# Values of two sequences loaded plainly by SyncE and cast by VectorE, in an attention kernel with a leaky-ReLU layer behind it

## The chip, the cores and the metric

The kernel runs on one core of one Trainium2 chip. The metric is the device time in microseconds (us) of one execution. The profile adds one execution taken by the hardware profiler. Its engines are TensorE (PE in the profile, with PEld for its weight loads), VectorE (DVE), ScalarE (ACT), GpSimd (POOL) and SyncE (SP). GpSimd and SyncE also issue transfers; their issues are instructions on their own in-order queues.

## What is computed

Attention over eight sequences of 576 tokens with eight heads of 64 values, each with 16 extra "beacon" keys and values that every token may see; then two matrix products with a leaky ReLU between them. Inputs and output are fp32.

```python
B, H, S, Nb, D = (8, 8, 576, 16, 64)
k_all = np.concatenate([beacon_k, k], axis=2)
v_all = np.concatenate([beacon_v, v], axis=2)
scores = np.matmul(q, k_all.transpose(0, 1, 3, 2)) / np.sqrt(D)
scores = np.where(causal, -1e9, scores)          # the beacon columns are never masked
a = softmax(scores)
x = np.matmul(a, v_all)                          # then heads side by side: 4608 x 512
h = x @ w_in                                     # 512 -> 2048
out = np.maximum(0.01 * h, h) @ w_out            # 2048 -> 512
```

## The kernel before

**Units of work.** A *pair* g is two heads of one sequence; g // 4 is the sequence, so pairs 0 to 3 belong to sequence 0, 4 to 7 to sequence 1, 8 to 11 to sequence 2. For each pair, TensorE makes the scores in transposed form (`score`, L256, for pairs 0 to 7; `block` and `stretch`, L299 and L774, in blocks of three 512-column tiles over all later pairs), ScalarE takes the exponential into `aT`, GpSimd blanks the upper triangle (`triangle`, L287), and TensorE multiplies with the values (`value`, two halves; L359). The values carry a column of ones, so the same product gives the sum that VectorE divides by (L388, L389) into `x_nat`. Two halves of a pair's value product: half 0 takes query tiles 0 to 2 and so key chunks 0 to 2; half 1 takes tiles 3 and 4 and all five chunks.

**Values.** `v_bufs` are two bf16 buffers, for even and odd sequences. `load_v_cast` (L205) fills one of five 128-row chunks with a transfer that GpSimd issues and that turns fp32 into bf16 on the way; chunk 0 takes a second small one for the 16 beacon rows. So a sequence takes six issues.

**Queries and keys.** Pairs 0 to 7 come in through `load_qk` (tile `gsum`) and are turned by TensorE. From pair 8 on, GpSimd loads them as `q_nat` and `k_nat` (`load_natural`, L167) and SyncE turns them by transposing transfers (`turn_pair`, L177), into `qT` and into the tile `kT`, which has eight key buffers. `beacon_columns` (L227) then copies the 16 beacon keys of a pair into the first columns of its key buffer, on GpSimd (L229).

**The layer behind.** Its input `xT` is filled by TensorE transposes and a copy (`finish`, L672, by way of `x_transposes`) or by SyncE's transposing transfers (`x_turn`, L412). The tokens are taken in nine chunks of 512. `up` makes one of 16 slices of the hidden layer (L442), which ScalarE writes to the tile `gT` (L450), of which there are two in turn; `down` makes a part of the output (L512 for chunk 0; L537 later). From chunk 1 on, the output product goes by sums of weight blocks (`weight_sums`, L455, three subtractions on VectorE) and of tokens (L610).

**What sets the order.** Each engine runs its instructions in the order in which the code issues them. For sequences 0 and 1 that order is written out by hand in strings that `run` (L680) reads (L739 to L758). A step is a letter and numbers: `s` a score tile, `m` its mask, `v` a value half, `x` a finish, `y` an `x_turn`, `q` and `k` turning by TensorE, `l` a `load_qk`, `N` a `load_natural` half, `T` a `turn_pair`, `V` a value chunk (`V1.0` is sequence 1, chunk 0), `i` and `o` halves of `w_in` and `w_out`, `b` a beacon copy, `t` the weight sums, `u` and `d` an `up` and a `down`. From sequence 2 on, events with a due time in units of pairs are sorted (L785 to L808) and slices of the layer are filled in between. Completion of transfers is counted on eight semaphores for GpSimd's and eight for SyncE's, used in turn, so an issue also waits until the eighth issue before it is done.

Of the kernel before, what the change touches and what calls it, by code (L numbers as in the profile page):

```python
# [8 lines left out]
FP32 = mybir.dt.float32  # L9
BF16 = mybir.dt.bfloat16  # L10
# [5 lines left out]
def kernel(  # L16
# [11 lines left out]
    nc = tc.nc  # L28

    B, H, S, D = q.shape  # L30
    NB = beacon_k.shape[2]
# [6 lines left out]
    NF = DF // 128  # L38
# [7 lines left out]
    NKB = 5  # L46
    ROWS = [128, 128, 128, 128, 80]
    OFF = [0, 112, 240, 368, 496]
# [31 lines left out]
    gpool = ctx.enter_context(tc.tile_pool(name="gpool", bufs=2))  # L80
# [21 lines left out]
    v_bufs = [singles.tile([128, NKB, H, D + 1], BF16, name=f"v_aug{i}") for i in range(2)]  # L102
# [102 lines left out]
    def load_v_cast(b, c):  # L205
        dst = v_bufs[b % 2]
        lo = 0
        if c == 0:
            nc.gpsimd.dma_start(
                out=dst[0:NB, 0, :, 0:D], in_=beacon_v[b].rearrange("h p d -> p h d")  # L210
            )
            lo = NB
        n = ROWS[c] - lo
        nc.gpsimd.dma_start(  # L214
            out=dst[lo : ROWS[c], c, :, 0:D],
            in_=v[b, :, OFF[c] : OFF[c] + n].rearrange("h p d -> p h d"),
        )

    def operand(g, which):
# [62 lines left out]
    def mask(g, part):  # L282
        aT = probs[g]
        for lo, n, rows in MASKS[part]:
            triangle(aT, lo, n, rows)
# [82 lines left out]
    def value_ahead(g):  # L368
        if (g, 0) not in avs:
            avs[g, 0] = ps_one.tile([128, 512], FP32, name="av", tag="one")  # L370
        value_matmuls(g, 0, avs[g, 0][:, 0:396].rearrange("p (n w) -> p n w", w=66), (0, 1))
        begun.add(g)
# [56 lines left out]
    gT = {}  # L429
# [242 lines left out]
    def finish(g, eng=0):  # L672
        if eng < 2 and g in xs:
            x_transposes(g, (dve, act)[eng])
        ready[0] = chunks_with(g)
        if g % NPAIR == NPAIR - 1:
            turn[0] = 1
            held[0] = LEAD

    def run(steps):  # L680
        for step in steps.split():
            op, a = step[0], [int(x) for x in step[1:].split(".")] if step[1:] else []
            if op == "s":
                score(*a)
            elif op == "m":
                mask(*a)
            elif op == "v":
                value(*a)
            elif op == "e":
                value_ahead(*a)  # L690
            elif op == "x":
                finish(*a)
            elif op == "l":
                load_qk(*a)
            elif op == "V":
                load_v_cast(*a)
            elif op == "N":
                load_natural(*a)
            elif op == "T":
                turn_pair(a[0])  # L700
            elif op == "y":
                x_turn(a[0])
            elif op == "q" or op == "k":
                t_q(a[0], 0 if op == "q" else 1, (dve, act)[a[1] if len(a) > 1 else 0])
            elif op == "b":
                beacon_columns(a[0], (dve, act, pool)[a[1]])
            elif op == "u":
                up()
            elif op == "d":
                down()  # L710
            elif op == "w":
                unused(*a)
            elif op == "W":
                unused_ahead(*a)
            elif op == "i":
                load_w_in(a[0])
            elif op == "o":
                load_w_out(a[0])
            elif op == "t":
                weight_sums(a[0])  # L720
            else:
                raise ValueError(step)
# [11 lines left out]
    with order:  # L734
        load_first_keys()
        load_beacon_k(0, 2, nc.scalar)
        nc.vector.memset(blank, 0.0)
        nc.vector.memset(ident, 0.0)
        run("l0.0 l1.0")  # L739
        make_identity(nc, ident, nomemset=True)  # L740
        make_ones()
        run("l1.1 l2.0 l2.1 V0.0 V0.1 l3.0 l3.1 V0.2 V0.3 V0.4 l4.0 l4.1 i0")
        make_pads()
        unused(13, 256)
        cast_beacon_k(0, 2, nc.scalar.copy)
        beacon_transposes(0, 2)
        unused(13)
        nc.scalar.copy(out=k_nat0[:, :, 0], in_=first_k[0])
        nc.vector.tensor_copy(out=k_nat0[:, :, 1], in_=first_k[1])
        run("q0.1 k0 w2.384 s0.0 m0.0 w3.256 s0.1 q1 s0.2 m0.1 k1 s0.3 m0.2")  # L750
        run("w2.384 s1.0 m1.0 q2 s1.1 k2 w2.384 s1.2 m1.1 w2.384 s1.3 m1.2 W0.0.4 s2.0 m2.0 W0.0.4 s2.1 W0.0.6 q3 l5.0 l5.1 s2.2 k3 w4.384 v0.0 m2.1 s2.3 i1 m2.2 W0.1.4 s3.0 m3.0 v1.0 s3.1 v0.1 s3.2 v1.1 m3.1 l6.0 l6.1 s3.3 x0.1 m3.2")
        run("v2.0 V1.0 V1.1 q4 v2.1 x1 k4.1 v3.0 v3.1 x2.1 s4.0 s4.1 x3 m4.0 V1.2 V1.3 V1.4 l7.0 l7.1 u u s4.2 s4.3 q5 k5 m4.1 m4.2 u o0 u")
        load_beacon_k(2, B, nc.gpsimd)
        run("s5.0 s5.1 m5.0 u u u s5.2 s5.3 q6 k6 m5.1 m5.2 o1 u u s6.0 s6.1 m6.0 u v4.0 u v4.1 y4 N8.0 N8.1 u s6.2 s6.3 q7 k7 m6.1 m6.2 u")
        cast_beacon_k(2, B, nc.gpsimd.tensor_copy)
        run("u v5.0 u v5.1 N9.0 s7.0 s7.1 m7.0 d x5 v6.0 v6.1 T8 d s7.2 s7.3")
        beacon_transposes(2, B)
        run("m7.1 m7.2 N9.1 u b8.2 b9.2 b10.2 b11.2 x6 v7.0 T9 v7.1 d d t0 d N10.0 N10.1 d V2.0 V2.1 x7 T10")  # L758


        FIRST = 2 * NPAIR
        COLS = FLAT[NKB]
        TILES = (NG - FIRST) * COLS // 512

        def tile_parts(n):
            at, end, parts = 512 * n, 512 * (n + 1), []
            while at < end:
                r, lo = divmod(at, COLS)
                hi = min(COLS, lo + end - at)
                parts.append((FIRST + r, lo, hi))  # L770
                at += hi - lo
            return parts

        def block(m):  # L774
            tiles = [tile_parts(n) for n in range(3 * m, min(3 * m + 3, TILES))]
            for n, parts in enumerate(tiles):
                stretch(parts, apart=n == 0)
            for parts in tiles:
                triangles(parts)

        def has_down():
            return at2[0] < done1[0] // NF

        since = 0
        events = []  # L785
        for g in range(FIRST, NG):
            if g > FIRST + 2:
                events.append((g - 2.75, 0, run, ("N%d.0" % g,)))
                events.append((g - 2.45, 0, run, ("N%d.1" % g,)))
            if g > FIRST + 2:  # L790
                events.append((g - 1.75, 0, run, ("T%d" % g,)))
            if g > FIRST + 3:
                events.append((g - 1.65, 0, run, ("b%d.2" % g,)))
            at = g + (2.05 if g % NPAIR == NPAIR - 1 else 2.25)
            events.append((at, 3, value, (g, 0)))
            events.append((at + 0.37, 4, value, (g, 1)))
            events.append((at + 0.38, 5, x_turn, (g,)))
        for m in range((TILES + 2) // 3):
            events.append((FIRST + (0.4 if m else 0.6) + 1536 / COLS * m, 2, block, (m,)))
        ends = [FIRST]  # L800
        for g in range(FIRST, NG):
            events.append((g + 3.5, 2, finish, (g, 2)))
            if g % NPAIR == NPAIR - 1:
                ends.append(g + 3.5)
        for b in range(2, B):
            for n in range(2 if b == 2 else 0, NKB):
                events.append((4 * b + (-0.4 if b == 2 else -0.9) + 0.3 * n, 6, load_v_cast, (b, n)))
        events.sort(key=lambda e: e[:2])  # L808
        first_down[0] = 4
        w, d0 = 0, done1[0] + done2[0]  # L810
        for at, _, what, args in events:
            while w + 2 < len(ends) and at > ends[w + 1]:
                w, d0 = w + 1, done1[0] + done2[0]
            todo = NF * ready[0] + sum(ND(i) for i in range(ready[0])) - KEPT - d0
            aim = d0 + todo * (at - ends[w]) / (ends[w + 1] - ends[w])
            while done1[0] + done2[0] < aim and fill():
                pass
            if what is block:
                since = done1[0] + done2[0]
            elif what is value:  # L820
                while done1[0] + done2[0] < since + (2 if has_down() else 4) and fill(True):
                    pass
            what(*args)
        while at2[0] < NCH:
            fill()
# [30 lines left out]
```

## Time and profile before

| | |
|---|---|
| three runs | 330.48, 332.94, 335.08 us |
| the profiled execution | 333.21 us, of which the profile's span is 331.5 |
| mean granted TensorE clock in it | 0.995 |
| values, issue to landing (128 KB chunks, median) | 7.1 us |
| keys and queries of a pair, issue to landing (72 KB, median) | 4.6 to 4.9 us |
| transposing transfers, issue to landing (median) | 4.6 to 4.8 us |

Two parts of the page:

```profile
ACT  4969862588753885477756784686467516553510
POOL 8795868979997697567748877697221000000000
PEclk9999999999997999999999999999999999999999
DMA  8999999999999999999999999999321111000103
...
q0 software_dynamic: 99824, 18.54, 85.2%
q1 hardware_dynamic: 55792, 20.77, 36.8%
```

The first four rows cut the span into 40 slices of 8.3 us; a digit is the busy share in tenths, or the granted clock. The other two rows are the transfer queues: q0 is fed by GpSimd, q1 by SyncE, and both run on the same 16 transfer engines; packets, megabytes and the time of the packets as a share of 16 engines. In the timelines quoted below, a line gives the start, the time taken, engine, source line and operation, how many instructions it merges, and in brackets the idle time of the engine before it and what ended it.

### The profile page before, as it was taken

How to read it: one execution, taken by the hardware profiler on the slowest of the kernel's cores; microseconds unless marked ns; L12 is line 12 of the kernel's file. 1: busy time of each engine (PE TensorE's matmuls, PEld its weight loads, DVE VectorE, ACT ScalarE, POOL GpSimd, SP SyncE). 2: the span in 40 equal slices, each digit the busy share in tenths (PEclk: the TensorE clock that was granted, in tenths of full speed). 3: DMA queues.
4: the chain of work that ended last, by engine and by line, in shares of the span. 5: the costliest groups of instructions: out<-in, count | busy, mean ns of one | idle time of the engine just before them, and what ended most of it. 6: DMA issues, size and time to landing. Idle time of an engine off the chain costs nothing.

```text
span 331.5 us, 8537 instructions
## 1 busy us (share of the span) xinstructions
PE 319.8 (96%) x3429; PEld 213.5 (64%) x3429; DVE 145.9 (44%) x297; ACT 200.1 (60%) x336; POOL 187.5 (57%) x354
## 2 busy tenths in 40 slices
PE   7999999899969999999999999999999999999995
PEld 4574555355657457855688888557865684566685
DVE  3563346307534254435434535443543552424344
ACT  4969862588753885477756784686467516553510
POOL 8795868979997697567748877697221000000000
PEclk9999999999997999999999999999999999999999
DMA  8999999999999999999999999999321111000103
GB/s 134 127 202 184 131 208 126 179 165 154 139 134 141 169 134 132 154 137 149 133 138 146 120 131 140 187 128 117 87 97 51 36 52 63 2 33 32 65 32 129
DMA packets 155928, 39.93 MB, mean 120 GB/s; under 512 B 143040, under 2 KB 153152, under 8 KB 155888
## 3 DMA queue, kind: packets, MB, share of 16 engines
q0 software_dynamic: 99824, 18.54, 85.2%
q1 hardware_dynamic: 55792, 20.77, 36.8%
q8 instruction: 27, 0.44, 0.6%
q14 instruction: 13, 0.11, 0.1%
q10 hardware_dynamic: 272, 0.07, 0.1%
HBM read 37.22 MB, written 9.44 MB: 141 GB/s over the span
## 4 chain that ended last, share of the span: by engine, by line
PE 67%; DMA 16%; ACT 4%; POOL 4%; DVE 4%; issue 3%; SPq 1%; DVEq 0%; ACTq 0%; POOLq 0%
PE acc L442 28%; PE acc L537 25%; PE av L359 6%; PE sc L314 5%; DMA gsum<-in_q_dram 5%; DMA xT<-x_nat 3%; DMA w_out_sb<-in_moe_w_out_dram 3%; DMA v_aug<-in_v_dram 3%; ACT aT L333 3%; PE acc L512 2%; DMA k_nat<-in_k_dram 2%; POOL aT L289 1%; DVE p L559 1%; DVE u L559 1%; POOL gsum L158 1%
## 5 line engine op out<-in xcount | busy, mean ns | idle before, releaser
L442 PE MATMUL acc<-xT,w_in_sb 128*128 128x512 bf16 (+1 forms) x640 | 136.8, 358 | 1.4 <-DMA xT<-x_nat 0.5
L450 ACT ACTIVATE gT<-acc 128x512 bf16<-128x512 f32 x144 | 83.5, 617 | 54.0 <-PE acc L442 51.5
L289 POOL TENSOR_SCALAR_AFFINE_SELECT aT<-aT 128x256 bf16<-128x256 bf16 (+2 forms) x160 | 64.0, 429 | 55.3 <-ACT aT L329 34.1
L442 PEld LDWEIGHTS <-w_in_sb 128*128 128x128 bf16 x640 | 59.4, 98 | 52.6 <-issue 4.2
L537 PEld LDWEIGHTS <-gT 128*128 128x128 bf16 x512 | 49.5, 99 | 9.1 <-issue 1.0
L333 ACT ACTIVATE aT<-sc 128x1024 bf16<-128x1024 f32 (+3 forms) x64 | 51.8, 895 | 2.0 <-PE sc L314 2.0
L537 PE MATMUL acc<-w_out_sb,gT 128*128 128x256 bf16 x384 | 47.9, 279 | 0.0
L359 PEld LDWEIGHTS <-aT 128*128 128x128 bf16 (+1 forms) x960 | 36.6, 98 | 9.4 <-DVE x_nat L389 1.5
L537 PEld LDWEIGHTS <-gsum 128*128 128x128 bf16 x384 | 36.7, 98 | 6.7
L359 PE MATMUL av<-v_aug,aT 128*128 128x65 bf16 (+1 forms) x960 | 39.5, 194 | 1.1 <-DVE x_nat L389 0.5
L329 ACT ACTIVATE aT<-sc 128x512 bf16<-128x512 f32 (+3 forms) x64 | 29.0, 522 | 18.4 <-PE sc L314 18.4
L562 ACT COPY p<-acc 128x512 f32<-128x512 f32 (+1 forms) x25 | 14.5, 581 | 41.2 <-PE acc L537 37.6
L388 DVE RECIPROCAL rec<-av 128x6 f32<-128x6 f32 (+1 forms) x64 | 11.9, 187 | 56.1 <-PE av L359 55.8
L214 POOL DMA_DIRECT2D v_aug<-in_v_dram x40 | 34.0, 855 | 4.1 <-DMA w_in_sb<-in_moe_w_in_dram 3.3
L171 POOL DMA_DIRECT2D k_nat<-in_k_dram x48 | 34.8, 729 | 1.0 <-issue 0.9
L171 POOL DMA_DIRECT2D q_nat<-in_q_dram x48 | 34.8, 731 | 0.7
L389 DVE TENSOR_TENSOR x_nat<-av,rec 128x384 bf16<-128x384 f32 (+1 forms) x64 | 31.4, 490 | 2.2
L537 PE MATMUL acc<-w_sum,gsum 128*128 128x256 bf16 x256 | 31.9, 273 | 0.0
L276 ACT ACTIVATE aT<-sc 128x1024 bf16<-128x1024 f32 (+3 forms) x32 | 26.0, 875 | 5.1 <-PE sc L267 5.0
L314 PE MATMUL sc<-qT,kT 64*128 64x80 bf16 (+22 forms) x384 | 22.2, 250 | 3.3 <-POOL kT L229 2.7
L610 DVE TENSOR_TENSOR gsum<-gT 128x1024 bf16<-128x1024 bf16 x16 | 11.2, 697 | 30.1 <-ACT gT L450 30.1
L314 PEld LDWEIGHTS <-kT 64*128 64x128 bf16 x384 | 13.0, 94 | 15.1 <-issue 8.7
(62 smaller groups left out, 225.1 us busy)
## 6 DMA issues: line engine op xcount, KB each, us to landing
out_dram<-p SPq DMA_DIRECT2D x26, 256.0 KB, 2.4
q_nat<-in_q_dram POOLq DMA_DIRECT2D x48, 72.0 KB, 4.6
k_nat<-in_k_dram POOLq DMA_DIRECT2D x48, 72.0 KB, 4.9
v_aug<-in_v_dram POOLq DMA_DIRECT2D x24, 128.0 KB, 7.1
w_in_sb<-in_moe_w_in_dram POOLq DMA_DIRECT2D x2, 1024.0 KB, 11.9
w_out_sb<-in_moe_w_out_dram POOLq DMA_DIRECT2D x2, 1024.0 KB, 11.7
out_dram<-u SPq DMA_DIRECT2D x8, 256.0 KB, 2.4
gsum<-in_q_dram POOLq DMA_DIRECT2D x8, 144.0 KB, 6.6
```

Source lines behind the costliest of these rows:

```text
L171: nc.gpsimd.dma_start(out=t[:, :, par], in_=(q, k)[which][b, 2 * hp + par].rearrange("(t p) d -> p t d", p=NR),)
L214: nc.gpsimd.dma_start(out=dst[lo : ROWS[c], c, :, 0:D], in_=v[b, :, OFF[c] : OFF[c] + n].rearrange("h p d -> p h d"),)
L276: nc.scalar.activation(out=aT[:, :, c0 : c0 + w], in_=sc[:, :, 0:w], func=AF.Exp, scale=0.125)
L289: nc.gpsimd.affine_select(out=view, in_=view, compare_op=ALU.is_ge, fill=0.0, base=128 - n if lo == 0 else 0, channel_multiplier=-1, patte ...
L314: nc.tensor.matmul(out=(sc[par] if apart else sc[:, par])[:, at : at + b - a], lhsT=kT[ps_, c * 128 : (c + 1) * 128], rhs=qT[ps_, q0 : q0 ...
L329: nc.scalar.activation(out=probs[g][:, par, lo:hi], in_=sc[par][:, at : at + hi - lo], func=AF.Exp, scale=0.125)
L333: nc.scalar.activation(out=probs[g][:, :, lo:hi], in_=sc[:, :, at : at + hi - lo], func=AF.Exp, scale=0.125)
L359: nc.tensor.matmul(out=avv[:, n, 0 : D + 1], lhsT=aT[0 : ROWS[c], par, a0 : a0 + 128], rhs=va[0 : ROWS[c], c, 2 * hp + par, :], start=(c = ...
L389: nc.vector.tensor_tensor(out=x_nat[:, t0:t1].rearrange("p t e d -> p (t e) d"), in0=avv[:, :, 0:D], in1=rec[:, n0:n1, None].to_broadcast( ...
L442: nc.tensor.matmul(out=acc[:, lo:hi], lhsT=w_in_cols(fc, j), rhs=xT[:, j, x0 : x0 + hi - lo], start=(j == 0), stop=(j == NJ - 1), skip_gro ...
L450: nc.scalar.activation(out=gT[i][:, fc, :], in_=acc, func=AF.Prelu, alpha=0.01)
L537: nc.tensor.matmul(out=acc[:, lo : lo + HD], lhsT=left(i, n, fc, tile), rhs=right(n, fc), start=(lo == 0 and fc == 0), stop=(fc == HF - 1) ...
```

## The change

The values of sequences 1 and 2 no longer come through `load_v_cast`. Five steps `L` (`load_v_plain`) have SyncE bring the fp32 values, unchanged in type, into `gT[1]`, the hidden-layer tile of chunk 1, which is not written before the end of the hand-written part; it is cut into eight staging places. A step `G` (`gate_v`) writes two zeros into each place on VectorE, and SyncE's load waits for that. Five steps `C` (`cast_v`) have VectorE copy the values into the bf16 buffer. Sequence 1 is gated behind `v3.0`, and cast behind `k6`; sequence 2 is gated behind `x5`, and cast at the end of the hand-written part.

Besides, one `u` moves from before `s6.2` to before `v4.0`, the weight sums `t0` and the finish `x7` change places so that `t0` stands behind `x7`, and a beacon copy is due 2.5 units before its pair rather than 1.65. Sequences 3 to 7 keep the old loads.

```diff
+    def gate_v(*slots):
+        for i in range(2):
+            if i not in gT:
+                gT[i] = gpool.tile([128, NF, 512], BF16, name="gT")
+        for n in slots:
+            nc.vector.memset(stage(n)[:, 0:1, 0:2], 0.0)
+
+    def stage(n):
+        return gT[1][:, 2 * n : 2 * n + 2].rearrange("p f t -> p (f t)").bitcast(FP32).rearrange(
+            "p (h d) -> p h d", d=D
+        )
+
+    def load_v_plain(b, c, n):
+        t = stage(n)
+        lo = 0
+        if c == 0:
+            nc.sync.dma_start(out=t[0:NB], in_=beacon_v[b].rearrange("h p d -> p h d"))
+            lo = NB
+        nc.sync.dma_start(
+            out=t[lo : ROWS[c]], in_=v[b, :, OFF[c] : OFF[c] + ROWS[c] - lo].rearrange("h p d -> p h d")
+        )
+        staged[b, c] = n
+
+    def cast_v(b, c):
+        nc.vector.tensor_copy(
+            out=v_bufs[b % 2][0 : ROWS[c], c, :, 0:D], in_=stage(staged[b, c])[0 : ROWS[c]]
+        )
...
-        run("v2.0 V1.0 V1.1 q4 v2.1 x1 k4.1 v3.0 v3.1 x2.1 s4.0 s4.1 x3 m4.0 V1.2 V1.3 V1.4 l7.0 l7.1 u u s4.2 s4.3 q5 k5 m4.1 m4.2 u o0 u")
+        run("v2.0 q4 v2.1 x1 k4.1 v3.0 G0.4.1.2.6 L1.0.0 L1.1.4 L1.2.1 L1.3.2 L1.4.6 v3.1 x2.1 s4.0 s4.1 x3 m4.0 l7.0 l7.1 u u s4.2 s4.3 q5 k5 m4.1 m4.2 u o0 u")
         load_beacon_k(2, B, nc.gpsimd)
-        run("s5.0 s5.1 m5.0 u u u s5.2 s5.3 q6 k6 m5.1 m5.2 o1 u u s6.0 s6.1 m6.0 u v4.0 u v4.1 y4 N8.0 N8.1 u s6.2 s6.3 q7 k7 m6.1 m6.2 u")
+        run("s5.0 s5.1 m5.0 u u u s5.2 s5.3 q6 k6 C1.0 C1.1 C1.2 C1.3 C1.4 m5.1 m5.2 o1 u u s6.0 s6.1 m6.0 u u v4.0 u v4.1 y4 N8.0 N8.1 s6.2 s6.3 q7 k7 m6.1 m6.2 u")
...
-        run("u v5.0 u v5.1 N9.0 s7.0 s7.1 m7.0 d x5 v6.0 v6.1 T8 d s7.2 s7.3")
+        run("u v5.0 u v5.1 N9.0 s7.0 s7.1 m7.0 d x5 G3.7.2.6.5 L2.0.3 L2.1.7 L2.2.2 L2.3.6 L2.4.5 v6.0 v6.1 T8 d s7.2 s7.3")
...
-        run("m7.1 m7.2 N9.1 u b8.2 b9.2 b10.2 b11.2 x6 v7.0 T9 v7.1 d d t0 d N10.0 N10.1 d V2.0 V2.1 x7 T10")
+        run("m7.1 m7.2 N9.1 u b8.2 b9.2 b10.2 b11.2 x6 v7.0 T9 v7.1 d d d N10.0 N10.1 d x7 t0 C2.0 C2.1 C2.2 C2.3 C2.4 T10")
...
-                events.append((g - 1.65, 0, run, ("b%d.2" % g,)))
+                events.append((g - 2.5, 0, run, ("b%d.2" % g,)))
...
-        for b in range(2, B):
-            for n in range(2 if b == 2 else 0, NKB):
-                events.append((4 * b + (-0.4 if b == 2 else -0.9) + 0.3 * n, 6, load_v_cast, (b, n)))
+        for b in range(3, B):
+            for n in range(NKB):
+                events.append((4 * b - 0.9 + 0.3 * n, 6, load_v_cast, (b, n)))
```

In the diff, a step's first number is the sequence or pair; the numbers of `G` and the last number of `L` are staging places. A pair of numbers behind `s`, `m` and `v` is pair and part.

More of the change, by code (lines that the diff above doesn't have):

```diff
@@ L216, in load_v_cast @@
             in_=v[b, :, OFF[c] : OFF[c] + n].rearrange("h p d -> p h d"),
+        )
+    staged = {}
+    def gate_v(*slots):
[21 more added lines that the diff above has]
+            out=v_bufs[b % 2][0 : ROWS[c], c, :, 0:D], in_=stage(staged[b, c])[0 : ROWS[c]]
         )
@@ L696, in run @@
                 load_v_cast(*a)
+            elif op == "G":
+                gate_v(*a)
+            elif op == "L":
+                load_v_plain(*a)
+            elif op == "C":
+                cast_v(*a)
             elif op == "N":
```

## The prediction, made before the changed kernel had run

> **What bounds the kernel now.** I read the page's busy times first, then the idle marks in TensorE's timeline, then for each mark what the queues did before it.
>
> ```profile
> PE 319.8 (96%) x3429; PEld 213.5 (64%) x3429; DVE 145.9 (44%) x297; ACT 200.1 (60%) x336; POOL 187.5 (57%) x354
> ```
>
> TensorE is idle for 331.5 - 319.8 = 11.7 us, of which the windows 0 to 10 and 300 to 331.5 us hold 1.9 and 3.3: start and tail. So at most about 6.5 us of idle can be won, and any new wait of TensorE, whose queue is in order, is paid in full. TensorE's timeline (start, duration, idle before, releaser), at the places that the edit touches:
>
> ```profile
> 38.35 0.53 PE L359 MATMUL av<-v_aug,aT 128*128 128x65 bf16 x12
> 39.59 0.72 PE L359 MATMUL av<-v_aug,aT 128*128 128x65 bf16 x18
> 47.10 1.04 PE L512 MATMUL acc<-w_out_sb,gT 128*128 128x512 bf16 x4 [0.70 <-DMA w_out_sb<-in_moe_w_out_dram]
> ...
> 60.04 0.38 PE L442 MATMUL acc<-xT,w_in_sb 128*128 128x512 bf16 x1 [0.44 <-DVE xT L410]
> 61.88 0.85 PE L314 MATMUL sc<-qT,kT 64*128 64x512 bf16 x12 [0.59 <-PE acc L512]
> ...
> 99.59 0.50 PE L314 MATMUL sc<-qT,kT 64*128 64x256 bf16 x6 [2.66 <-POOL kT L229]
> 100.02 3.57 PE L537 MATMUL acc<-w_out_sb,gT 128*128 128x256 bf16 x16
> ```
>
> The first two lines are the first value products of sequence 1 (v4.0, v4.1): they read the values that the change reroutes. The last wait has a tail: 16 products take 3.57 us where 16 of the same line take 1.91 at 88.38, and the granted clock from 100 to 110 us is 0.83, so it costs 2.66 + 1.66 = 4.3 us. Its releaser is misnamed: the beacon copy that ends at 99.56 is pair 15's, but these matmuls read pair 14's keys, whose copy ran at 94.66. What lands just before 99.59 is pair 14's key transpose, issued at 92.77:
>
> ```profile
> kT<-k_nat SPq DMA_TRANSPOSE x1, 6.7
> ```
>
> 92.77 + 6.7 = 99.47. At 61.88 it is the same: pair 8's key transpose went out at 56.74 and took 5.0, to 61.74.
>
> GpSimd's timeline, where the rerouted loads stand now:
>
> ```profile
> 23.17 0.61 POOL L158 DMA_DIRECT2D gsum<-in_k_dram  x1
> ...
> 24.94 1.85 POOL L214 DMA_DIRECT2D v_aug<-in_v_dram  x2
> ...
> 27.30 1.77 POOL L214 DMA_DIRECT2D v_aug<-in_v_dram  x2
> 32.32 0.73 POOL L214 DMA_DIRECT2D v_aug<-in_v_dram  x1 [3.25 <-DMA w_in_sb<-in_moe_w_in_dram]
> 33.99 0.60 POOL L158 DMA_DIRECT2D gsum<-in_q_dram  x1 [0.94 <-DMA gsum<-in_q_dram]
> ...
> 36.80 0.78 POOL L137 DMA_DIRECT2D w_out_sb<-in_moe_w_out_dram  x1
> ```
>
> Last the DMA queues (packets, MB, share) in three windows: 31 to 34, 39 to 43 and 47 to 50 us.
>
> ```profile
> q0 software_dynamic: 2719, 0.38, 370.7%
> ```
> ```profile
> q0 software_dynamic: 400, 0.80, 109.6%
> ...
> xT<-x_nat SPq DMA_TRANSPOSE x2, 12.0
> ```
> ```profile
> q0 software_dynamic: 267, 0.55, 95.4%
> q1 hardware_dynamic: 265, 0.07, 17.1%
> ```
>
> GpSimd's queue (q0) alone moves 906 small packets a us (values), or 100 large ones (w_out). Where SyncE's queue (q1) stands beside w_out, the two go one packet for one, 88 and 89 a us, though q1's packets are small. That is why the two x transposes issued at 41.02 and 42.36 took 12 us: the first packets show at 45, about 4 us after issue. This decides my forecast.
>
> **The change part by part.**
>
> *Sequence 1's values on SyncE.* They are 592 rows x 8 heads = 4736 packets (the windows from 30 to 36 us hold 4753). Now they stand in q0 ahead of w_out and are through by 36. After the change they are issued when VectorE reaches the five memsets, behind the normalisation that ends at 25.3: SyncE from 25.4, packets from 29.4 by the x transposes' delay.
>
> GpSimd loses the six issues, with them the 3.25 us wait, and pair 7's loads no longer wait for a completion slot. So w_out's first half goes out after the masks that wait for ScalarE's exp (ended 30.0), about 30.9 instead of 36.8. It has no further use for being early (TensorE asks at 46.4), and it now flows while the values should.
>
> Count the values' packets, one for one with q0. From 29.4 to 30.4, the tail of w_in and pair 6: 88. Pair 7's two loads, 2 x 128 packets: 256, to about 32.5. Then q0 is empty until w_out is at full rate, 2.3 us after issue in this trace (36.8 to 39), so until 33.2: 0.7 us at 906, 630. Sum 970 (340 without the gap, 1300 if packets flow at once). W_out's first half, 512 packets at 89 a us, to 39.0: 1480. The beacon keys, 768 small packets, half of the 1025 a us that both queues reach together from 60 to 62 us, to 40.5: 2250. W_out's second half, issued about 36.5: 512 more, to 46.3: 2760. Then only small packets, 512 a us each: 3072 (chunks 0 to 2, v4.0) at 46.9, 4096 at 48.9, 4736 at 50.2; with 340 or 1300 in place of 970 the last is 51.4 or 49.5. About 1 us for completion and up to 0.66 for the cast (0.745 us for 64x576 from fp32 at L749, times 512/576) make 51.8, and v4.1 ends near 52.0. Now it ends at 40.3; with the one `u` moved ahead of v4.0 (0.87) it would be 41.2. **New wait: 10.8 us (9.8 to 12).** Behind it on TensorE stands everything; on VectorE the casts stand ahead of pair 4's normalisation and of pair 7's copies, which TensorE reaches later still. After the wait the clock dips as at 100 us: +1.7 (0 to 3.3, there are two waits).
>
> The Trainium skill, "DMA: Bandwidth & Descriptors", section on queues, rings and completion order, says that an engine takes turns between queues by packets of some 9 to 17 descriptors. If those were 9 to 17 of the value rows for each w_out packet, 296 rows per engine would need about 23 turns and be in before 34 us, with no wait at all; the 265 against 267 above does not show such turns for transposes, and no plain load beside w_out is in this trace.
>
> *Casts, ten on VectorE.* Up to 0.66 each, 3.3 for five. With the values late the first five are part of the wait; in time, they end before 39.5 and v4.0 stands at 39.2: nothing. The second five stand with the weight sums (3.7 us) between pair 7's copy and p4's copy, which frees a bank for block 1's scores (66.2 now): 57.5 + 3.7 + 3.3 = 64.5, hidden by 1.7; without that cover they cost up to 3.3. Where VectorE works between two SBUF operands, GpSimd's masks stretch: five take 3.57 us at 88.96 and 1.73 at 96.23, so a cast may hold GpSimd. The same skill's "SBUF — State Buffer" calls this an exclusive lock that an fp32 copy takes; five casts then hold GpSimd for 3.3 us. GpSimd is idle 1.9 us between 72 and 76 and loses 4.8 us of issues here (0.53, 2.62, 0.92 and 0.73 between 58 and 67), so I take nothing (0 to +1).
>
> *Sequence 2's values on SyncE* stand ahead of the transposes of pairs 8 to 10. Six issues at 0.6 (1.21 for two plain loads at the start) and 4736 packets at 512 to 906 a us: 5 to 9 us, and 1 to 2 for pair 8's own 2 x 576 rows. After the wait pair 5's finish comes near 60 (48.9 now), so pair 8's keys land at 67 to 72; TensorE asks at 72.7 (61.3 now). Nothing, at worst +2.
>
> *Weight sums behind pair 7's finish:* the 0.44 at 60.04 goes. *W_out early:* the 0.70 goes. *The beacon copy one pair earlier:* 0.2 us on GpSimd, and the 2.66 us wait is not its: nothing. GpSimd's 4.8 us of freed time does not carry on to pair 14 either, since it waits for ScalarE's exp at 75.1 before it starts the full stretch to 104.
>
> Sum on the profiled run: 331.5 + 10.8 + 1.7 - 0.44 - 0.70 = 342.9 us of span; 333.21 - 331.5 = 1.7 lies around it: **344.6**. That run is 0.3 above the median, 332.94, so 344.3.
>
> **The rivals.** A, *the values arrive in time.* A plain load may keep more packets in flight than a transpose. Needed: 4736 packets from 29 to 39.5, 450 a us; q1 reaches 471 alone in one window at 56. Against it: 88 beside w_out. Then 331.5 - 0.44 - 0.70 + 0.2 (pair 8's keys behind the second values) = 330.6, time 332.3. It turns into my forecast below 450 a us.
>
> B, *faster: GpSimd's relief goes all the way.* If k_nat of pair 14 is issued 3 us earlier (85.8 now), its transpose, the wait at 99.59 with its clock, the 0.53 for x at 108.3 and the 0.59 all go: 331.5 - 0.44 - 0.70 - 0.59 - 4.32 - 0.53 = 324.9, time 326.6. It decides where GpSimd enters the stretch at 75.6 with fewer than its present tasks; the three waits for ScalarE just before speak against it.
>
> C, *the change does only half:* SyncE's loads issue later than 25.4 because the memsets wait; each us later costs at most one us more. It is within my range.
>
> **How the numbers follow.** The late values 0.70, A 0.17, B 0.13. A measurement of this kernel tells about 2%, 6.7 us, from no change. The forecast's own range is 341 to 350: 9.8 of wait and no dip give 341.6; 12, with 3.3 of dip, 2 for pair 8 and 1 for GpSimd, give 350. Reaching down to A (332.3, less the spread of 2.4 below the median that the runs of now show) leaves out B and a tail: 329 to 350. Faster 0.12, same 0.18, slower 0.70.
>
> **What would show it.** Idle before v4.0 and v4.1 (L359, then L389) of about 7 and 4 us, ended by VectorE's casts, which end their own idle by SyncE's loads; these loads 20 to 25 us from issue to landing; w_out issued near 31; q1 and q0 one for one from 33 to 39. The wait at 47.10 and the 0.44 gone, the one before pair 14's scores still there. The forecast is wrong if the plain loads land by 38: q1 above 450 packets a us beside w_out.

## The result, and the profile after

| | median | runs |
|---|---|---|
| before | 333.69 us | 6, 330.48 to 338.51 |
| after | 347.43 us | 6, 344.79 to 351.91 |

The change makes the kernel slower: 1.0394 times the time before, 95% interval 1.0313 to 1.0475. The prediction was 344.3 us (329 to 350). The profiled execution took 350.68 us, 3.3 above the median, with a span of 348.8; a second profile of the same kernel has the same span and nearly the same waits (the first experiment). The ratios, and the times given with the experiments, leave out executions in a slower state, over 1.5% above the fastest of their kernel; of the others the median is 332.94 us before and 346.08 after.

The page after, the rows that answer to those shown of before:

```profile
PE 323.0 (93%) x3402; PEld 216.2 (62%) x3429; DVE 149.8 (43%) x317; ACT 200.4 (57%) x336; POOL 178.2 (51%) x342
...
PEclk9999955999999989999999999999999999999999
DMA  9999993499999999999999999999931212000203
...
q0 software_dynamic: 90160, 17.33, 71.3%
q1 hardware_dynamic: 65456, 23.20, 38.2%
```

The span grew by 17.3 us. TensorE's idle time went from 11.7 to 25.8 (14.1 more), its busy time from 319.8 to 323.0 (3.2 more, the same products at a lower clock: slices 6 and 7, from 44 to 61 us, have 5 of 10). The trace lacks 27 of the products (3402 of 3429), and their time stands as idle, so the two parts are not exact. 9664 packets went from GpSimd's queue to SyncE's.

TensorE's timeline after, at the same places:

```profile
39.23 0.26 PE L389 MATMUL av<-v_aug,aT 128*128 128x65 bf16 x3
48.35 0.43 PE L389 MATMUL av<-v_aug,aT 128*128 128x65 bf16 x5 [8.86 <-DVE v_aug L245]
50.80 0.38 PE L389 MATMUL av<-v_aug,aT 128*128 128x65 bf16 x4 [2.02 <-DVE v_aug L245]
...
53.31 1.14 PE L389 MATMUL av<-v_aug,aT 128*128 128x65 bf16 x15 [0.26 <-DVE v_aug L245]
...
62.41 1.04 PE L542 MATMUL acc<-w_out_sb,gT 128*128 128x512 bf16 x4
...
77.47 0.85 PE L344 MATMUL sc<-qT,kT 64*128 64x512 bf16 x12 [1.58 <-DMA kT<-k_nat]
...
114.09 0.50 PE L344 MATMUL sc<-qT,kT 64*128 64x256 bf16 x6 [1.31 <-DMA kT<-k_nat]
...
123.94 0.39 PE L472 MATMUL acc<-xT,w_in_sb 128*128 128x512 bf16 x1 [3.29 <-DMA xT<-x_nat]
```

v4.0 starts on the first chunk at 39.2, then waits 8.86 for the second and 2.02 for the third; v4.1 waits only 0.26 more. Together 11.1 us. W_out no longer waits (62.41 has no mark), nor does x7. Pair 8's keys are late by 1.58 us (0.59 before), pair 14's by 1.31 (2.66), and xT by 3.29 at 123.94 (0.53 before, at 108.32).

SyncE's timeline (its issues), then GpSimd's two issues of w_out:

```profile
25.45 22.38 SPq L239 DMA_DIRECT2D gT<-in_v_dram  x5
...
64.65 5.07 SPq L239 DMA_DIRECT2D gT<-in_v_dram  x5
...
71.45 1.23 SPq L179 DMA_TRANSPOSE kT<-k_nat  x1
```
```profile
30.39 0.76 POOL L137 DMA_DIRECT2D w_out_sb<-in_moe_w_out_dram  x1
...
36.75 0.77 POOL L137 DMA_DIRECT2D w_out_sb<-in_moe_w_out_dram  x1
```

The second column is the news: five issues of sequence 1 keep SyncE for 22.4 us, those of sequence 2 for 5.1. Here an issue of up to 1024 short rows isn't over when it is handed in; SyncE stays in it, and everything behind it in SyncE's queue stands still.

The queues (packets, MB, share) in the windows 31 to 34, 33 to 39 and 41 to 45 us:

```profile
q0 software_dynamic: 333, 0.38, 86.2%
q1 hardware_dynamic: 694, 0.17, 42.1%
```
```profile
q0 software_dynamic: 592, 1.11, 97.9%
q1 hardware_dynamic: 536, 0.13, 15.0%
```
```profile
q0 software_dynamic: 492, 0.82, 110.8%
q1 hardware_dynamic: 97, 0.02, 4.0%
```

While w_out starts, the values pass two packets for one of GpSimd's queue; over the window that the forecast names it is nearly one for one, and later one for five.

### The profile page after: what moved, and what is told of

It is laid out like the page before. It is cut to its first block, busy times and chain, and to the rows that moved or that the text cites. A ratio compares the mean times of both kernels' runs of the same rounds, so it can differ in the third digit from the quotient of the medians.

```text
span 348.8 us, 8533 instructions
## 1 busy us (share of the span) xinstructions
PE 323.0 (93%) x3402; PEld 216.2 (62%) x3429; DVE 149.8 (43%) x317; ACT 200.4 (57%) x336; POOL 178.2 (51%) x342
## 4 chain that ended last, share of the span: by engine, by line
PE 72%; DMA 17%; DVE 3%; ACT 3%; POOL 2%; issue 2%; SPq 0%; DVEq 0%; ACTq 0%; POOLq 0%
PE acc L472 31%; PE acc L567 24%; DMA gT<-in_v_dram 8%; PE av L389 7%; PE sc L344 5%; DMA kT<-k_nat 3%; PE acc L542 3%; DMA v_aug<-in_v_dram 3%; DMA k_nat<-in_k_dram 2%; ACT aT L363 2%; DMA xT<-x_nat 1%; POOL gsum L158 1%; DVE u L589 1%; PE sc L297 1%; DVE p L589 1%
## 5 line engine op out<-in xcount | busy, mean ns | idle before, releaser
L472 PE MATMUL acc<-xT,w_in_sb 128*128 128x512 bf16 (+1 forms) x617 | 138.9, 365 | 5.3 <-DMA xT<-x_nat 3.3
L472 PEld LDWEIGHTS <-w_in_sb 128*128 128x128 bf16 x640 | 60.5, 99 | 59.3 <-issue 8.9
L567 PEld LDWEIGHTS <-gT 128*128 128x128 bf16 x512 | 48.8, 98 | 8.3 <-issue 1.0
L389 PE MATMUL av<-v_aug,aT 128*128 128x65 bf16 (+1 forms) x960 | 41.0, 196 | 12.4 <-DVE v_aug L245 11.1
L389 PEld LDWEIGHTS <-aT 128*128 128x128 bf16 (+1 forms) x960 | 37.7, 99 | 21.3 <-issue 15.3
L567 PE MATMUL acc<-w_out_sb,gT 128*128 128x256 bf16 x384 | 46.2, 273 | 0.1
L418 DVE RECIPROCAL rec<-av 128x6 f32<-128x6 f32 (+1 forms) x64 | 11.9, 187 | 58.2 <-PE av L389 58.0
L214 POOL DMA_DIRECT2D v_aug<-in_v_dram x30 | 25.7, 862 | 0.1
## 6 DMA issues: line engine op xcount, KB each, us to landing
w_in_sb<-in_moe_w_in_dram POOLq DMA_DIRECT2D x2, 1024.0 KB, 12.1
gT<-in_v_dram SPq DMA_DIRECT2D x6, 256.0 KB, 12.5
```

The source lines that it names most:

```text
L214: nc.gpsimd.dma_start(out=dst[lo : ROWS[c], c, :, 0:D], in_=v[b, :, OFF[c] : OFF[c] + n].rearrange("h p d -> p h d"),)
L389: nc.tensor.matmul(out=avv[:, n, 0 : D + 1], lhsT=aT[0 : ROWS[c], par, a0 : a0 + 128], rhs=va[0 : ROWS[c], c, 2 * hp + par, :], start=(c = ...
L472: nc.tensor.matmul(out=acc[:, lo:hi], lhsT=w_in_cols(fc, j), rhs=xT[:, j, x0 : x0 + hi - lo], start=(j == 0), stop=(j == NJ - 1), skip_gro ...
L567: nc.tensor.matmul(out=acc[:, lo : lo + HD], lhsT=left(i, n, fc, tile), rhs=right(n, fc), start=(lo == 0 and fc == 0), stop=(fc == HF - 1) ...
```

## The experiments

Twelve runs; each ratio is to the kernel before on the same chip, with its 95% interval. In the timelines quoted, start and duration come first, and brackets hold the idle time before.

**The changed kernel again.** No edit.

> The changed kernel once more, as a yardstick for the kernels beside it. Theory: about 346 us, two waits of TensorE before sequence 1's value products, 11 us in sum, both ended by VectorE's casts that wait for SyncE's loads, and the granted clock at 0.5 for some us behind them. If the profile of the changed kernel was an odd one, the waits or the time behind them with a halved clock come out shorter.

349.3 us (348.01, 350.59; ratio 1.0449, 1.0337 to 1.0560). Waits of 9.38, 2.09 and 0.20 before the values, 2.77 before pair 8's scores, 2.96 before xT. So the profile of the changed kernel is no odd one, though the time is 3 us above the 346 expected.

**One sequence back at a time.** First sequence 1's values back on GpSimd, its V steps at their old places:

```diff
- v2.0 q4 v2.1 x1 k4.1 v3.0 G0.4.1.2.6 L1.0.0 L1.1.4 L1.2.1 L1.3.2 L1.4.6 v3.1
+ v2.0 V1.0 V1.1 q4 v2.1 x1 k4.1 v3.0 v3.1
...
- x3 m4.0 l7.0
+ x3 m4.0 V1.2 V1.3 V1.4 l7.0
...
- k6 C1.0 C1.1 C1.2 C1.3 C1.4 m5.1
+ k6 m5.1
```

> Sequence 1's values go by GpSimd again, sequence 2's stay on SyncE with their casts, and the moved weight sums and beacon copy stay. Theory (the late values of sequence 1 are the whole loss): the two waits are gone, the 0.44 us wait for xT is gone, the 0.70 us wait for w_out is back; 331 to 334 us. Rival (the second set of loads and casts, behind weight sums on VectorE and ahead of the transposes on SyncE, costs as well): 335 us or more, with a wait of over 1.5 us before pair 8's scores or block 1's.

344.58 us, ratio 1.0336 (1.0244 to 1.0428): the rival holds, and my theory, that sequence 1's values are the whole loss, falls. SyncE's and TensorE's timelines:

```profile
48.41 12.10 SPq L239 DMA_DIRECT2D gT<-in_v_dram  x5
...
63.10 1.42 SPq L179 DMA_TRANSPOSE kT<-k_nat  x1
```
```profile
68.88 1.48 PE L344 MATMUL sc<-qT,kT 64*128 64x512 bf16 x12 [9.24 <-DMA kT<-k_nat]
```

Sequence 2's loads are issued at 48 here, beside the end of w_out and GpSimd's loads of pairs 8 to 10, and hold SyncE for 12.1 us. Pair 8's key transpose goes out at 63.10 where it went at 56.74 before, and TensorE waits 9.24. So sequence 2 costs 10 us alone. In the changed kernel the first wait moves its loads to 64.65, when GpSimd's queue is quiet (no packet of it from 62 to 70 us), and so hides them.

Then sequence 2's values back on GpSimd, the last three chunks as events again:

```diff
- x5 G3.7.2.6.5 L2.0.3 L2.1.7 L2.2.2 L2.3.6 L2.4.5 v6.0
+ x5 v6.0
...
- d x7 t0 C2.0 C2.1 C2.2 C2.3 C2.4 T10
+ d V2.0 V2.1 x7 t0 T10
```

> Sequence 2's values go by GpSimd again, sequence 1's stay on SyncE. Theory: the two waits stay as they are, so 344 to 347 us, within 2 us of the changed kernel. Rival (sequence 2's share of the loss is several us): 341 us or less.

349.55 us, ratio 1.0444 (1.0365 to 1.0522): the waits before the values stay (11.5 us), and nothing is won: the changed kernel itself is at 349.3 on this chip. So sequence 1 costs 15 us alone, sequence 2 10, and both together 15. The costs don't add.

**W_out held.** Its first half is issued just ahead of its second:

```diff
- m4.1 m4.2 u o0 u
+ m4.1 m4.2 u u
...
- m5.1 m5.2 o1 u u
+ m5.1 m5.2 o0 o1 u u
```

> The changed kernel, but GpSimd issues the first half of w_out directly before the second half, about 6 us later, where nothing of it is wanted before TensorE reaches the output product. Theory (w_out's packets take every second turn from SyncE's): the values land by 38 to 41 us, the wait before the first value product falls from 9 us to under 2, and the time is 332 to 337 us, if w_out itself is not late by then. Rival (256-byte rows that SyncE's queue fetches are slow by themselves, or other traffic of GpSimd's queue holds them): still 8 us or more of waiting, 344 us or more.

343.86 us, ratio 1.0284 (1.0202 to 1.0367). By its numbers the rival nearly holds (7.92 us of waiting, it asked for 8), but the trace says something else. VectorE, TensorE, and the queues from 40 to 46 us:

```profile
47.98 0.43 DVE L245 CAST v_aug<-gT 80x512 bf16<-80x512 f32 x1 [8.19 <-DMA gT<-in_v_dram]
```
```profile
48.46 0.49 PE L389 MATMUL av<-v_aug,aT 80*128 80x65 bf16 x6 [7.92 <-DVE v_aug L245]
```
```profile
q0 software_dynamic: 526, 1.05, 94.6%
q1 hardware_dynamic: 522, 0.13, 16.6%
```

Four chunks are cast by 39.8. The fifth, 640 packets, meets w_out (issued at 36.30) and passes one for one, 522 against 526: 8 us for 160 KB. SyncE is held for 11.9 us instead of 22.4. The hold was too short.

**W_out behind the values.** Sequence 2 on GpSimd, and both halves of w_out behind pair 6's first mask:

```diff
- m4.1 m4.2 u o0 u
+ m4.1 m4.2 u u
...
- m5.1 m5.2 o1 u u s6.0 s6.1 m6.0 u u v4.0
+ m5.1 m5.2 u u s6.0 s6.1 m6.0 o0 o1 u u v4.0
```

> Sequence 2's values by GpSimd, sequence 1's on SyncE, and both halves of w_out issued behind pair 6's first mask, about 2 us later than in the run where they were held. Theory (with w_out held, only the last chunk's 640 rows met w_out's packets): sequence 1's last cast ends by 41 us and the wait before its value product is under 2 us; w_out is now the late one, 3 to 5 us at the first output product; 335 to 339 us. Rival (the last chunk is slow for another reason): the cast ends after 45 us, 343 us or more.

336.77 us, ratio 1.0100 (1.0063 to 1.0137). VectorE and TensorE:

```profile
39.47 0.96 DVE L245 CAST v_aug<-gT 128x512 bf16<-128x512 f32 x2 [0.58 <-DMA gT<-in_v_dram]
```
```profile
47.66 1.04 PE L542 MATMUL acc<-w_out_sb,gT 128*128 128x512 bf16 x4 [1.60 <-DMA w_out_sb<-in_moe_w_out_dram]
```

Against the run with only sequence 2 put back, w_out's later start (both halves at 38.55) takes away all waiting before the values; w_out itself is 1.60 late, less than I gave it. What is left are 2.38 us before scores at 73.87 and 2.49 before xT at 109.44.

**Long rows.** The changed kernel, with other rows in SyncE's loads:

```diff
-            out=t[lo : ROWS[c]], in_=v[b, :, OFF[c] : OFF[c] + ROWS[c] - lo].rearrange("h p d -> p h d")
+            out=t[lo : ROWS[c]].rearrange("p h d -> p (h d)"),
+            in_=v[b].rearrange("h (p r) d -> (h p) (r d)", r=8)[OFF[c] : OFF[c] + ROWS[c] - lo],
```

> The changed kernel, but SyncE's loads take the same bytes of sequences 1 and 2 as 592 rows of 2 KB instead of 592 x 8 rows of 256 bytes; tokens and heads then stand in other places of the tile, so the values that are multiplied are not in the reference's order. Theory (beside w_out SyncE's queue gets one packet for each of GpSimd's, so the number of packets decides and not the bytes): sequence 1 is in by 39 us, the waits before v4.0 and v4.1 fall under 1.5 us in sum, SyncE is held under 8 us by its loads instead of 22, pair 8's keys are in time; 330 to 336 us. Rival (the bytes, or SyncE's queue standing behind GpSimd's, decide): 6 us or more of waiting before the values, 341 us or more.

332.43 us, ratio 0.9958 (0.9914 to 1.0001), for a kernel whose output is not the function's, since tokens and heads stand in other places. SyncE's and TensorE's timelines (in this execution the matmuls of the first 24 us ran about 1.6 times as long, at a granted clock of 1.00, so that everything stands some 6 us later):

```profile
31.57 2.40 SPq L239 DMA_DIRECT2D gT<-in_v_dram  x5
```
```profile
45.07 0.53 PE L390 MATMUL av<-v_aug,aT 128*128 128x65 bf16 x12
...
111.96 0.61 PE L473 MATMUL acc<-xT,w_in_sb 128*128 128x512 bf16 x1 [4.65 <-DMA xT<-x_nat]
```

The same bytes in an eighth of the packets hold SyncE for 2.4 us, land 3 to 6 us after issue, and nobody waits for values or for pair 8's keys. The number of packets was the cost, of both sequences. This run doesn't show how long rows share with w_out, which goes out at 36.50: from 33 to 38 us 600 of their packets pass beside 159 of GpSimd's queue, so they are nearly in before it flows. With both costs gone, the one large wait left is that for xT.

**Sequence 2 early.** Sequence 1 on GpSimd; sequence 2's loads behind k6, at 36 us:

```diff
- q6 k6 C1.0 C1.1 C1.2 C1.3 C1.4 m5.1
+ q6 k6 G3.7.2.6.5 L2.0.3 L2.1.7 L2.2.2 L2.3.6 L2.4.5 m5.1
...
- v4.1 y4 N8.0 N8.1 s6.2 s6.3
+ v4.1 N8.0 N8.1 s6.2 s6.3 x4
...
- x5 G3.7.2.6.5 L2.0.3 L2.1.7 L2.2.2 L2.3.6 L2.4.5 v6.0
+ x5 v6.0
...
- v7.1 d d d N10.0 N10.1 d x7 t0 C2.0 C2.1 C2.2 C2.3 C2.4 T10
+ v7.1 C2.0 C2.1 C2.2 C2.3 C2.4 d d d N10.0 N10.1 d x7 t0 T10
```

> Sequence 1's values by GpSimd; sequence 2's on SyncE, but gated behind k6 at about 36 us instead of behind x5 at 48, so that SyncE has issued them before pair 8's keys are to be turned; pair 4's x is turned by TensorE (x4 for y4), and the casts stand behind v7.1. Theory (what costs is that SyncE is held in the issue of plain loads while transposes stand behind them, not the load or the cast): SyncE is free by 52 to 56 us, the 9 us wait before pair 8's scores falls under 1.5 us, 329 to 334 us. Rival (the bytes or the casts cost wherever they stand): 337 us or more.

339.78 us, ratio 1.0195 (1.0140 to 1.0250): the rival's time, but the trace fits neither text whole. VectorE and TensorE:

```profile
61.03 0.43 DVE L245 CAST v_aug<-gT 80x512 bf16<-80x512 f32 x1 [0.90 <-DMA gT<-in_v_dram]
...
61.97 0.44 DVE L440 COPY xT<-tp 128x576 bf16<-128x576 bf16 x1
```
```profile
62.47 0.38 PE L472 MATMUL acc<-xT,w_in_sb 128*128 128x512 bf16 x1 [3.75 <-DVE xT L440]
65.61 1.48 PE L344 MATMUL sc<-qT,kT 64*128 64x512 bf16 x12 [1.74 <-DMA kT<-k_nat]
```

SyncE was held from 36.2 to 53.9 (17.7 us beside w_out), free in time as expected, and pair 8's wait fell from 9.24 to 1.74. But the last chunk landed at 61, and the casts, which I had put ahead of x7's copy, held VectorE's queue for it: a new wait of 3.75. Another of 3.66 stands before xT at 113.35.

**The beacon copy alone,** on the kernel before:

```diff
-                events.append((g - 1.65, 0, run, ("b%d.2" % g,)))
+                events.append((g - 2.5, 0, run, ("b%d.2" % g,)))
```

> The kernel before with the beacon copies due 2.5 units before their pair, nothing else. Theory (the 2.66 us wait before pair 14's scores ends with pair 14's key transpose, not with a beacon copy): the wait stays between 2.2 and 2.8 us, the time within 1.5 us of the kernel before. Rival (the copy was the releaser): the wait is gone with its slow clock, 4 us less, about 329.

333.53 us, ratio 1.0015 (0.9975 to 1.0054): no difference that can be measured. TensorE:

```profile
96.47 0.76 PE L314 MATMUL sc<-qT,kT 64*128 64x256 bf16 x6 [1.83 <-DMA kT<-k_nat]
...
106.34 0.38 PE L442 MATMUL acc<-xT,w_in_sb 128*128 128x512 bf16 x1 [1.69 <-DMA xT<-x_nat]
```

The wait stays, now with its true releaser's name; 1.83 + 1.69 = 3.52 stands where 2.66 + 0.53 = 3.19 stood. I had expected the first number to keep its size.

**Fillers in the wait.** Products on zeros ahead of v4.0 and v4.1, added work that nothing reads:

```diff
- u u v4.0 u v4.1
+ u u w40.384 v4.0 u w10.384 v4.1
```

> The changed kernel, with 40 products of 384 columns on zeros, which nothing reads, ahead of v4.0 and 10 ahead of v4.1, so that TensorE works through most of the time in which it would wait. Theory (the waits also cost a halved clock behind them, 3 to 4 us): the granted clock stays at 1.0 from 44 to 60 us, and the time falls by 2 to 4 us against the changed kernel, to 343 to 346. Rival (the clock comes down for another reason, or what runs at the low clock waits for something else anyway): within 1 us of the changed kernel or above it.

350.12 us, ratio 1.0499 (1.0452 to 1.0547): no gain over the changed kernel's 349.3, which was taken on another chip. One of the windows of 2 us, with the granted clock third from the end (it is 1.00 in the one before), and TensorE's timeline:

```profile
50.00:52.00 2.00, 0.88 (x6) 0.47 (x6) 0.43 (x1) 0.00 (x0) 0.00 (x0) 0.52 0.44 64
```
```profile
53.00 3.41 PE L675 MATMUL av<-blank 128*128 128x384 bf16 x10
56.20 1.04 PE L389 MATMUL av<-v_aug,aT 128*128 128x65 bf16 x18
```

The first 40 took 6.7 us and kept the clock at 1.00 until 50; the 2.94 and 2.02 us of waiting that were left brought it down all the same, and the ten at half speed took 3.41 us and made v4.1 later. The first output product starts at 62.40, in the changed kernel at 62.41: what the clock gave back, the ten had cost. Yet the run prices the clock. From the end of v4.1 to the first output product it needs 62.40 - 57.24 = 5.16 us at full clock (1.00 from 57 us on), the kernel before 47.10 - 0.70 - 40.31 - 0.87 = 5.22 (without w_out's wait and the moved `u`), the changed kernel 62.41 - 54.45 = 7.96. The low clock costs 2.7 us there.

**X first on SyncE.** The changed kernel, with the transposes of every fourth pair behind x's:

```diff
-                events.append((g - 1.75, 0, run, ("T%d" % g,)))
+                events.append((g - (1.5 if g % NPAIR == NPAIR - 1 else 1.75), 0, run, ("T%d" % g,)))
```

> The changed kernel, with the key and query transposes of the fourth pair of each later sequence due 1.5 units before the pair instead of 1.75, so that on SyncE they stand behind the x transposes of four pairs earlier. Theory (the 3 us wait for xT at 124 us ends late because the x transposes stand behind pair 15's key transpose, which waits for a load that GpSimd issues late): that wait falls under 0.6 us, with it its dip of the clock; 343 to 345 us. Rival (x itself is late there): the wait stays, within 1 us of the changed kernel.

344.67, 336.85, 344.72, 343.45 us, too uneven for a ratio. The edit touches nothing ahead of pair 11, yet in this profile SyncE was held 10.6 us instead of 22.4, and TensorE waited 9.2 before the values instead of 11.1; the run of 336.85 us has a mean granted clock of 0.999 where the others have 0.978 to 0.980, so it can hardly have had such a wait, but no profile of it was kept. What the two queues do to each other differs from one execution to the next. The wait for xT is down to 0.24, and one for pair 15's keys stands three us later:

```profile
117.50 0.39 PE L472 MATMUL acc<-xT,w_in_sb 128*128 128x512 bf16 x1 [0.24 <-DMA xT<-x_nat]
...
120.44 0.45 PE L344 MATMUL sc<-qT,kT 64*128 64x128 bf16 x6 [2.05 <-DMA kT<-k_nat]
```

**Orders alone, on the kernel before:** weight sums behind x7, the edit just shown, and

```diff
-                events.append((4 * b + (-0.4 if b == 2 else -0.9) + 0.3 * n, 6, load_v_cast, (b, n)))
+                events.append((4 * b + -0.4 + 0.3 * n, 6, load_v_cast, (b, n)))
```

> The kernel before with orders alone changed: weight sums behind x7, the same later place of the fourth pair's transposes, and the values of sequence 3 and later due half a unit later, behind the keys of the pair that TensorE waits for at 99.6 us. Theory (that wait hangs on GpSimd's queue, 0.53 + 0.83 + 0.90 us of value issues stand ahead of pair 14's keys, and its tail at the low clock is paid too): the wait falls under 0.6 us, the waits of 0.44 and 0.53 for xT are gone, 327 to 330 us, faster than both. Rival (GpSimd's masks and SyncE's order give it back, as the beacon copy's move did): the waits come up within 10 us of there, 332 us or more.

332.19 us, ratio 0.9954 (0.9923 to 0.9984): the fastest kernel of the study that computes the whole, by half a per cent, but the rival's time and not the 327 to 330 of the theory. TensorE:

```profile
95.00 0.50 PE L314 MATMUL sc<-qT,kT 64*128 64x256 bf16 x6 [0.20 <-DMA kT<-k_nat]
...
104.26 0.72 PE L314 MATMUL sc<-qT,kT 64*128 64x128 bf16 x6 [2.00 <-DMA kT<-k_nat]
```

Pair 14's 2.66 is down to 0.20, as the theory had it, and 2.00 comes up nine us later, at pair 15's keys, as the rival had it.

**The change repaired:** sequence 1 on SyncE with w_out behind it, sequence 2 on GpSimd, and the two later orders of the last run.

> The changed kernel repaired by what the runs showed: sequence 2's values by GpSimd, sequence 1's on SyncE with w_out behind them (pair 6's first mask), and the two later orders of the run before (fourth pair's transposes behind x, later values behind the keys). It asks whether the change's idea, taking loads from GpSimd, is worth anything once its waits are gone. Theory (GpSimd's time before 75 us does not carry to its full stretch behind): no better than those orders alone on the kernel before, 331 to 335 us, with 1 to 2 us of waiting left for w_out. Rival (it carries): no wait over 1 us between 80 and 115 us, below 330 us.

332.95 us, ratio 1.0007 (0.9971 to 1.0043): 1.93 us of waiting for w_out at 47.46, 2.04 for pair 15's keys at 107.48. Taking sequence 1's loads from GpSimd is worth nothing that can be measured.

## Why the prediction was right, step by step

*Sequence 1's values, 10.8 us.* 11.1 measured (11.7 in the second profile), but 10.9 of it before v4.0 and 0.3 before v4.1, instead of about 7 and 4; v4.1 ended at 54.45, not 52.0. SyncE issued at 25.45 (25.4) and GpSimd w_out at 30.39 (30.9). That w_out's packets are the cause is shown: with w_out behind the values, the wait is gone; with an eighth of the packets, which are nearly in before w_out flows, too. *One for one* was right as a rate, 536 to 592 from 33 to 39 us and 522 to 526 in the run with w_out held, but not at each moment: 694 to 333, then 97 to 492. By 34 us 1832 of SyncE's packets had passed where the count has some 1040, by 45 us 3026 where it has some 2650, by 50 us 4630 where it has some 4650. The early lead was lost again, so that the sum came out within 0.3 us is in part luck. The 1 us for completion in that sum has no row behind it; the last 200 packets or so took 3 us, and the loads took 9 to 24 us from issue to landing, not 20 to 25. The rule of the Trainium skill ("DMA: Bandwidth & Descriptors", on queues, rings and completion order), a turn of some 9 to 17 descriptors, would have had the values in before 34 us; once w_out flows, no window here shows such turns for plain loads of 256-byte rows.

*The clock, 1.7 us.* This is the term that was mis-sized: 4.9 measured, outside its 0 to 3.3. Behind v4.1 the low clock costs 2.7 by the comparison above. Ahead of it, from 39.23 to 54.45, TensorE waits 11.14 us and works 4.08, where the same products take 1.96 in the kernel before (38.35 to 40.31): 2.1 more. The granted clock, third from the end, in two windows of 1 us and two of 10 us of the changed kernel:

```profile
43.00:44.00 1.00, 0.00 (x0) 0.00 (x0) 0.00 (x0) 0.00 (x0) 0.00 (x0) 0.73 1.13 211
60.00:61.00 1.00, 1.00 (x11) 0.58 (x9) 0.49 (x2) 0.41 (x1) 0.00 (x0) 0.74 0.97 62
```
```profile
40.00:50.00 10.00, 0.43 (x5) 0.32 (x5) 0.43 (x1) 0.40 (x1) 2.30 (x4) 0.67 1.26 190
50.00:60.00 10.00, 8.72 (x85) 4.91 (x86) 3.88 (x9) 2.79 (x5) 2.93 (x6) 0.50 0.29 34
```

It is 0.50 from about 43.5 to 60.5 us. The row used for the size, 1.66 behind a wait of 2.66 us, was too short a wait for one of 11. The Trainium skill ("TensorE: Matmul & The Clock Gate", what's actually happening) puts the fall behind an idle window of about 3.4 us; here 2.94 and 2.02 with little between them were enough (the filler run).

*Sequence 2 on SyncE, nothing, at worst +2.* 1.58 against 0.59, so 1.0, in bounds, because the first wait moved its loads to a quiet time. The step counted on the move, but not on what it was worth: its six issues, at 0.6 us each, took 5.4 us here and 12.5 where sequence 1 is back on GpSimd, because SyncE stays in them, and there the same loads cost 9.24 us of waiting and the kernel is at 344.6.

*So rival A was mispriced.* It had 332.3 us if the values arrived in time, with 0.2 for sequence 2. With sequence 1 back on GpSimd its values are in time, and the kernel is at 344.6 all the same. The rival's price needed short loads of both sequences: with long rows the time is 332.4. (The 471 packets a us that it calls q1's alone passed beside 249 of GpSimd's queue.)

*Casts, nothing.* They took 0.43 us each, not 0.66. In the changed kernel none ran beside a mask of GpSimd's, so whether a cast holds GpSimd isn't shown. Where they stand ahead of other work on VectorE they cost more by waiting (3.75 in the run with sequence 2 early) than by working.

*X7 and w_out,* -0.44 and -0.70: both waits are gone. *The beacon copy,* nothing: right, and its wait's true releaser is shown by name in the run with the copy alone.

*GpSimd's freed time doesn't carry on:* right, but not as I said. Pair 14's and xT's waits are 3.19 in sum before and 1.31 + 3.29 = 4.60 after. I took the wait for pair 14's keys as a fixed 2.66. As I read the traces it is one delay that GpSimd's full stretch (10.0 of 10 us busy from 80 to 90 and from 90 to 100 in the kernel before) hands down SyncE's queue, in which key transposes wait for GpSimd's loads and x transposes wait behind them. That is argued, not shown; what is shown is that the beacon copy's move, the x-first order, the orders alone and the repaired change moved waits between pair 14, xT and pair 15, and none took them away.

In sum: the forecast of 344.3 missed the median of 347.4 by 3.1 us, and its span of 342.9 the profiled 348.8 by 5.9. Of these, 3.2 are the clock, 1.0 pair 8, 1.4 pair 14 and xT, 0.3 the first wait, which is the whole. (The slow tail that stood behind pair 14 before, 1.66, stands behind xT now: the products at 125.03 take 4.45 us, at 109.39 before 2.77.) The profiled execution is one of the longer ones; the six have mean granted clocks of 0.966 to 0.985, and it has 0.971, so the clock may cost less in others.

## What to carry to other kernels

Count a transfer's packets, not its bytes, and ask which queue's packets run beside it: 4608 rows of 256 bytes cost the kernel 10 to 15 us where the same bytes as 576 rows of 2 KB cost none. A load of many short rows holds the engine that issues it, so look for what stands behind it there, and for what stands behind its consumer. A cost that another wait hides comes back when that wait is repaired: take the parts out one at a time, and expect each to look worthless or decisive by what is left in.

## What the runs showed of the hardware that I had not expected

- SyncE's issue of five loads of 4608 rows lasted 22.4 and 17.7 us beside w_out, 12.1 beside its end and GpSimd's loads of keys and queries, 5.1 with GpSimd's queue quiet, and 2.4 us where the rows were 576 long ones.
- The share of SyncE's queue swung from two for one (31 to 34 us) to one for five (41 to 45 us), and ended in a trickle: from 50 to 53 us, 190 packets of SyncE's and 136 of GpSimd's queue, 109 a us, where 906 a us of GpSimd's alone pass in the kernel before (31 to 34 us). No view here shows packets by transfer engine, so the cause stays open.
- TensorE's clock fell at the end of two waits of 2.94 and 2.02 us with 0.3 us of work between them (the filler run), and came back only at about 57 us, some 6 us after work had resumed at 51.1. In the changed kernel it fell at about 43.5, 4 us after the work before the first wait had ended, and came back at about 60.5, nearly 10 us after work had resumed at 50.8.
